# One plan of slots for the attention work between the matmuls of blocks 1 to 6

## The chip, the cores and the metric

The kernel runs on one NeuronCore of one Trainium2 chip. The metric is the device time of one execution in microseconds (us). The core has TensorE (PE, the matmuls; PEld is its weight load), VectorE (DVE), ScalarE (ACT), GpSimd (POOL, which here issues the large loads) and SyncE (SP, which here issues transposing DMAs). PSUM is the memory that matmuls write into; it is handed out in pieces called banks.

## The reference, cut to what matters

Two stages follow each other. Linear attention with a cosine weight (8 batches, 8 heads, 576 tokens, head size 64) makes the 4608 x 512 input `x` of a mixture of 8 expert MLPs, of which every token takes all eight, weighted by a normalised routing matrix.

```python
q_p = phi(q, cos_w, sin_w); k_p = phi(k, cos_w, sin_w)   # relu, times cos and sin: 64 -> 128 features
kv  = einsum('bhsf,bhsd->bhfd', k_p, v)                  # "key sums"
z   = sum(k_p, axis=2)                                   # also from the key sums
num = einsum('bhsf,bhfd->bhsd', q_p, kv)
den = einsum('bhsf,bhf->bhs', q_p, z) + 1e-6
attn_out = num / den
# x = attn_out as 4608 x 512
P = exp(x @ w_gate ...); 8 rounds of row and column normalisation
out = sum over e of P[:, e] * (relu(x @ w1[e]) @ w2[e])
```

## The kernel before

While TensorE computes expert 0 for the tokens that are ready, the attention for the next tokens is woven in between. A block `j` is 512 tokens of expert 0: 16 slots, slots 0 to 7 one part of the first layer (`ffn1`, four matmuls of 128x512, about 0.87 us), slots 8 to 15 half a tile of the second (`ffn2`, the same size). After the matmuls of a slot the pieces of attention listed for it are written. The order in which instructions are written is the order on each engine: TensorE, VectorE and ScalarE each run their list in order, and a piece that has to wait holds up all that stands behind it on its engine (the trace of block 3 below shows it: `zsel` starts only at 123.58 us, behind VectorE's earlier pieces).

```python
for slot in range(NS):                      # NS = 16
    ... ffn1(hT, w0, j, [slot])  or  ffn2(...)
    for fn, args in todo.get((j, slot), []):
        fn(*args)
```

In block `j`, batch `b = j + 1` is finished and batch `b + 1` prepared. The pieces, by head pair `hk` (four of them):

```python
def prep_k(b, hk):  # ScalarE: relu(k) in place
def prep_q(b, hk):  # VectorE: relu(q), q_p = q * (cos, sin); from batch 2 on SyncE transposes it by DMA:
        qTs[b, hk] = q_pTs[(b * HK + hk) % len(q_pTs)]
        nc.sync.dma_start(out=qTs[b, hk], in_=q_p[:]..., transpose=True)
def prep_kv(b, hk): # VectorE: k_p = k * (cos, sin), and a copy of v into v_aug
def sums(b, half):  # TensorE: 36 small matmuls k_p x v_aug for two head pairs, into two banks; then sums_made
def sums_made(b, half, kv_ps):
    for hh in range(2):
        ve.tensor_tensor(out=zsel..., in0=zmask..., in1=kv_v[..., D : D + 1]..., op=ALU.mult)   # VectorE reads the bank
        se.copy(out=kv_sb..., in_=kv_v[:, :, 0:D])                                           # ScalarE reads the bank
def denominators(b):# TensorE: 24 matmuls zsel x qT, then VectorE: add, reciprocal, two splits -> hl
def attend(b, hk):  # TensorE: rb_ps = spread(hl) -> ScalarE copies to rb; num_ps = kv_sb x qT -> VectorE: xT = num_ps * rb
def gates(j):       # TensorE: x @ w_gate, ScalarE: exp
def load(b, half, names, held_back)  # GpSimd issues the loads of q, k, v; held_back: not before VectorE's last piece so far
```

All PSUM tiles of these pieces come from one pool of four banks, `small_ps`, taken in turn: two for `sums`, one for `denominators`, four for an `attend`. The plan before had one scheme for blocks 1 and 2 and another from block 3 on:

```python
elif b < B:
    if j <= 2:
        at(j, 0, prep_q, b, 3); at(j, 1, prep_kv, b, 3)
        at(j, 1, sums, b, 0);   at(j, 3, sums, b, 1)
        ...
    else:
        at(j, 0, sums, b, 1)
    at(j, 5 if j <= 2 else 4, denominators, b)
    for hk in range(HK):
        at(j, 8 + 2 * hk, attend, b, hk)
if j:
    at(j, 6, gates, j)
if j <= 1:
    ... load(b + 1, half) at slots 2 * half; prep of b + 1 from slot 6 on, except the fourth q and the fourth k, v
elif b + 1 < B:
    for slot, fn, hk in ((4, prep_k, 0), (5, prep_q, 0), (6, prep_kv, 0), ... (9, prep_q, 3), ... (12, prep_kv, 3)):
        at(j, slot, fn, b + 1, hk)
    at(j, 10, sums, b + 1, 0)
if 1 <= j and b + 2 < B:
    for half in range(2):
        at(j, 10 + half, load, b + 2, half, "qkv", True)
```

`kv_sb` and `zsel` are the two results of a key sum: `kv`, for the numerators, and `z`, masked by head, for the denominators. `rb` holds one over the denominators, spread out, and `xT` the finished attention.

(The `turn` pieces of the printed kernel do nothing from batch 2 on, which is all that these lines reach.)

The softmax here doesn't subtract the row's maximum and nothing guards it: scores larger than these inputs give would overflow.

## Time and profile before

The median is 1005.67 us (1005.21 to 1006.58); the profiled run has a span of 1005.6 us.

| what | before |
|---|---|
| TensorE busy, share of the span | 97% |
| TensorE's share of the chain of waits | 91% |
| blocks 1, 2, 3, 4, 5, 6 | 21.24, 31.49, 21.33, 21.34, 21.33, 18.76 us |
| mean granted clock in block 1, block 2, blocks 3 to 6 | 0.92, 0.84, 1.00 |

The blocks are cut at the first `ffn1` matmul of each in the timeline; only block 1 is cut at its third, the first one after its wait for `xT` (its first stands at 52.29 us). First, two parts of the page: the busy times, and the granted clock of TensorE in 40 slices of 25 us.

```profile
PE 974.6 (97%) x7846; PEld 681.4 (68%) x7846; DVE 810.0 (81%) x1838; ACT 566.3 (56%) x1260; POOL 60.3 (6%) x82
...
PEclk8997999999999999999999999999999999999999
```

The fourth slice (75 to 100 us) stands at 7. The windows view gives one row for each block: stretch, length, then busy time and instructions of PE, PEld, DVE, ACT, POOL, and last the mean clock, the share of the DMA engines and GB/s. Here are blocks 1 to 4.

```profile
53.77:75.01 21.24, 20.89 (x206) 10.09 (x206) 14.48 (x33) 12.42 (x28) 3.41 (x5) 0.92 0.41 61
75.01:106.50 31.49, 23.77 (x241) 11.38 (x240) 17.42 (x41) 13.04 (x32) 4.38 (x7) 0.84 0.82 121
106.50:127.83 21.33, 19.91 (x209) 10.15 (x208) 14.03 (x33) 12.80 (x29) 4.43 (x8) 1.00 0.84 139
127.83:149.17 21.34, 19.92 (x206) 10.06 (x204) 14.03 (x33) 12.79 (x29) 4.31 (x7) 1.00 0.81 139
```

Block 2 is 10 us longer than its neighbours, and blocks 3 and 4 have 1.4 us each in which TensorE has nothing to do. The waits view (engine, line, what it waited for: total us, times, longest) of TensorE up to 195 us names the two largest. L109 is the line of the helper that records every instruction, so one goes by the tiles; `acc_lo<-q_p` and `acc_hi<-q_p` are transposing DMAs of q into two pieces of borrowed storage.

```profile
PE small_ps L109 <- DMA acc_lo<-q_p: 6.4, 1, 6.4
PE small_ps L109 <- ACT kv_sb L109: 4.2, 4, 1.2
...
PE small_ps L109 <- DMA acc_hi<-q_p: 0.5, 1, 0.5
```

The long one is in block 2. The timeline of TensorE there (start, length, engine, instruction, count; in brackets the idle time before it):

```profile
81.85 0.51 PE L109 MATMUL small_ps<-q_pT,zsel 128*32 128x192 f16 x12
88.73 0.51 PE L109 MATMUL small_ps<-acc_lo,zsel 128*32 128x192 f16 x6 [6.38 <-DMA acc_lo<-q_p]
89.72 0.51 PE L109 MATMUL small_ps<-acc_hi,zsel 128*32 128x192 f16 x6 [0.47 <-DMA acc_hi<-q_p]
90.16 1.89 PE L109 MATMUL h_ps<-xT,w1e 128*128 128x512 f16 x4
```

Half of the denominators is done, the rest waits for the transposes of the third (`acc_lo`) and fourth (`acc_hi`) head pairs. SyncE's timeline shows when these were issued, the third just before block 2 begins and the fourth in it:

```profile
74.86 3.24 SPq L339 DMA_TRANSPOSE acc_lo<-q_p  x1
78.27 6.15 SPq L339 DMA_TRANSPOSE acc_hi<-q_p  x1
```

The last row of TensorE's timeline shows the after-effect: four matmuls of 128x512 take 1.89 us, where the usual four take 1.03 as this view counts. What the transposes met is in the DMA view, for issues between 74 and 76 us (last figure: us from issue to landing):

```profile
q_ld<-in_q_dram POOLq DMA_DIRECT2D x1, 288.0 KB, 10.2
k_ld<-in_k_dram POOLq DMA_DIRECT2D x1, 288.0 KB, 12.5
v_ld<-in_v_dram POOLq DMA_DIRECT2D x1, 288.0 KB, 13.4
acc_lo<-q_p SPq DMA_TRANSPOSE x1, 13.8
```

The fourth pair's transpose takes 11.4 us. In block 3 the same transpose as in the last row lands after 3.3 us. The other wait recurs in every block from 2 to 5. In block 3, VectorE, ScalarE and TensorE around 124 us:

```profile
122.55 0.75 DVE L109 TENSOR_TENSOR k_p<-k_ld,acc_hi 128x1152 f16<-128x1152 f16 x1
123.21 0.45 DVE L109 COPY acc_lo<-v_ld 128x576 f16<-128x576 f16 x1
123.58 0.34 DVE L109 TENSOR_TENSOR zsel<-acc_hi,small_ps 128x64 f16<-128x64 f16 x2
...
123.82 0.43 ACT L109 CAST kv_sb<-small_ps 128x128 f16<-128x128 f32 x2 [3.82 <-DVE zsel L109]
...
124.14 0.44 PE L109 MATMUL small_ps<-q_pT,kv_sb 128*64 128x384 f16 x4 [1.21 <-ACT kv_sb L109]
```

VectorE is late with `zsel`, ScalarE's copy waits for `zsel`, and TensorE's `attend` for that copy. The `kv_sb` that the `attend` reads is the one of the current batch, long there; what it lacks is the PSUM bank, which is that of the next batch's key sums.

### The profile page before, as it was taken

The numbers are of one execution on the slowest core, as the hardware profiler recorded it, in microseconds if no ns is written. First come the engines' busy times: TensorE is split into PE (matmuls) and PEld (weight loads), VectorE is DVE, ScalarE is ACT, GpSimd is POOL, SyncE is SP. The second block draws the span as 40 slices with busy tenths as digits, with TensorE's granted clock in tenths as the row PEclk, the third lists the DMA queues.
The fourth block names the chain that finished last, engine by engine and source line by source line (L and its number), as shares of the span: only waits on it lengthen the run. The fifth ranks groups of instructions, "written<-read, shape, count | busy, mean of one in ns | idle before, by whom it ended". The sixth has DMA issues, their size and how long they took to land.

```text
span 1005.6 us, 20219 instructions
## 1 busy us (share of the span) xinstructions
PE 974.6 (97%) x7846; PEld 681.4 (68%) x7846; DVE 810.0 (81%) x1838; ACT 566.3 (56%) x1260; POOL 60.3 (6%) x82
## 2 busy tenths in 40 slices
PE   7997999999999999999999999999999999999997
PEld 7543444445777777777777777777777777777775
DVE  5875665488989887898889878888889888988886
ACT  5653566547777555555555555555555555555551
POOL 6310220001000000000000000000000000000001
PEclk8997999999999999999999999999999999999999
DMA  9947885353101331034013321043113410104535
GB/s 167 205 76 112 143 143 95 71 103 66 49 24 34 81 66 48 25 66 90 25 33 65 61 65 30 24 91 66 30 43 67 83 32 25 48 24 108 132 87 124
DMA packets 80336, 73.54 MB, mean 73 GB/s; under 512 B 33264, under 2 KB 72176, under 8 KB 80240
## 3 DMA queue, kind: packets, MB, share of 16 engines
q0 software_dynamic: 27232, 30.94, 19.5%
q1 hardware_dynamic: 52768, 41.06, 16.6%
q8 instruction: 61, 1.00, 0.4%
q14 instruction: 35, 0.29, 0.1%
q10 hardware_dynamic: 240, 0.26, 0.1%
HBM read 83.12 MB, written 12.98 MB: 96 GB/s over the span
## 4 chain that ended last, share of the span: by engine, by line
PE 91%; DVE 4%; DMA 2%; ACT 1%; issue 1%; POOL 1%; DVEq 0%; POOLq 0%; ACTq 0%; SPq 0%
PE rows_ps L109 33%; PE h_ps L109 27%; PE copied_ps L109 11%; PE p_ps L109 11%; PE y_ps L109 5%; PE small_ps L109 4%; DMA acc_hi<-q_p 1%; DVE xT L109 1%; DMA k_ld<-in_k_dram 1%; DVE k_p L109 1%; DVE den L109 0%; DVE acc_lo L109 0%; ACT rb L109 0%; DVE acc_hi L819 0%; POOL hs_last L834 0%
## 5 line engine op out<-in xcount | busy, mean ns | idle before, releaser
L819 DVE SCALAR_TENSOR_TENSOR acc_lo<-rows_ps,P_tok,acc_lo 128x512 f32<-128x512 f32 (+1 forms) x322 | 203.3, 640 | 74.6 <-PE rows_ps L109 74.5
L109 PEld LDWEIGHTS <-H 128*128 128x128 f16 x2080 | 203.0, 98 | 83.1 <-issue 1.2
L755 ACT CAST u<-h_ps 128x384 f16<-128x384 f32 x288 | 137.8, 478 | 130.6 <-PE h_ps L109 130.0
L109 PEld LDWEIGHTS <-w1e 128*128 128x128 f16 x1632 | 157.0, 98 | 69.1 <-issue 8.8
L749 DVE CUSTOM_DVE_ANT_0 H<-p_ps,u 128x384 f16<-128x384 f32 x329 | 181.2, 551 | 6.7 <-PE p_ps L109 6.5
L109 PEld LDWEIGHTS <-hs 128*128 128x128 f16 x1500 | 146.6, 98 | 56.2
L109 PE MATMUL h_ps<-S,w1e 128*128 128x384 f16 x672 | 164.1, 326 | 1.1 <-ACT u L109 0.9
L109 PE MATMUL p_ps<-xT,T 128*128 128x384 f16 x672 | 164.1, 326 | 0.1
L109 PE MATMUL h_ps<-xT,w1e 128*128 128x384 f16 (+1 forms) x616 | 152.6, 356 | 1.3 <-DVE xT L109 1.2
L109 PE MATMUL rows_ps<-V,H 128*128 128x256 f16 x1000 | 150.0, 273 | 0.7 <-DVE acc_hi L819 0.7
L109 PE MATMUL rows_ps<-w2e,hs 128*128 128x256 f16 x1000 | 150.0, 273 | 0.0
L787 ACT ACTIVATE H<-h_ps 128x384 f16<-128x384 f32 x144 | 70.7, 491 | 95.1 <-PE h_ps L109 95.1
L109 PEld LDWEIGHTS <-T 128*128 128x128 f16 x1008 | 98.1, 98 | 29.2 <-issue 2.8
L109 PE MATMUL rows_ps<-w2e,H 128*128 128x256 f16 (+1 forms) x568 | 91.2, 285 | 0.0
L768 ACT COPY copied_ps<-h_ps 128x384 f32<-128x384 f32 x144 | 67.4, 468 | 35.6 <-PE h_ps L109 35.4
L778 ACT ACTIVATE H<-copied_ps 128x384 f16<-128x384 f32 x144 | 70.9, 492 | 20.3 <-PE copied_ps L109 20.3
L109 PE MATMUL h_ps<-S,T 128*128 128x384 f16 x336 | 81.8, 325 | 0.3 <-ACT copied_ps L109 0.3
L109 PE MATMUL copied_ps<-xT,w1e 128*128 128x384 f16 x336 | 82.1, 326 | 0.0
L109 PE MATMUL copied_ps<-w2e,H 128*128 128x256 f16 x504 | 75.5, 272 | 0.0
L109 PE MATMUL rows_ps<-V,hs 128*128 128x256 f16 x500 | 74.9, 272 | 0.0
L819 DVE SCALAR_TENSOR_TENSOR acc_lo<-copied_ps,P_tok,acc_lo 128x256 f32<-128x256 f32 x126 | 60.2, 477 | 0.4
L819 DVE SCALAR_TENSOR_TENSOR acc_hi<-rows_ps,P_tok,acc_hi 128x512 f32<-128x512 f32 (+1 forms) x56 | 41.3, 737 | 20.1 <-PE rows_ps L109 19.3
(135 smaller groups left out, 962.9 us busy)
## 6 DMA issues: line engine op xcount, KB each, us to landing
S<-x_saved SPq DMA_DIRECT2D x108, 192.0 KB, 2.4
out_dram<-acc_lo SPq DMA_DIRECT2D x62, 128.0 KB, 2.4
w1e<-in_moe_w_dram POOLq DMA_DIRECT2D x7, 1024.0 KB, 9.0
w2e<-in_moe_w_dram POOLq DMA_DIRECT2D x7, 1024.0 KB, 9.6
k_ld<-in_k_dram POOLq DMA_DIRECT2D x16, 288.0 KB, 8.5
v_ld<-in_v_dram POOLq DMA_DIRECT2D x16, 288.0 KB, 9.4
q_ld<-in_q_dram POOLq DMA_DIRECT2D x16, 288.0 KB, 8.6
x_saved<-S SPq DMA_DIRECT2D x18, 192.0 KB, 1.9
```

The costliest lines, as they stand in the source:

```text
L109: i = getattr(self.engine, name)(*args, **kwargs)
L749: latest = ve._custom_dve(TENSOR_ADD_SAT, out=out, in0=ps[:, 0:TU], in1=t[:], s0=FP32_MAX, s1=0.0)
L755: se.copy(out=t[:], in_=ps[:, 0:TU])
L768: se.copy(out=Y[:, 0:TU], in_=X[:, 0:TU])
L778: se.activation(out=h11, in_=Y[:, 0:TU], func=AF.Relu)
L787: se.activation(out=h12, in_=X[:, 0:TU], func=AF.Relu)
L819: ve.scalar_tensor_tensor(out=a, in0=rows, scalar=P_tok[:, g, self.e : self.e + 1], in1=a, op0=ALU.mult, op1=ALU.add,)
```

## The change

One scheme of slots for blocks 2 to 6, and a variant one slot later for the preparation in block 1. Batch 3 is now wholly prepared in block 1, and its first key sum taken there at slot 15. Key sums of the next batch stand at slot 14, behind all attends (before: 10), and at slot 0; denominators at slot 3 (before: 4, in block 2: 5), attends at 6, 8, 10, 12 (before: 8 to 14), gates at 5, held-back loads at 11 and 12. In `sums_made` ScalarE reads first. One more line, left out below, moves the loads of the second half of batch 3 from slot 2 of block 1 to slot 0. The work is the same.

```diff
@@ sums_made
             for hh in range(2):
+                se.copy(out=kv_sb[:, 2 * half : 2 * half + 2, hh, :], in_=kv_v[:, :, 0:D])
                 ve.tensor_tensor(out=zsel[...], in0=zmask[...], in1=kv_v[...], op=ALU.mult)
-                se.copy(out=kv_sb[:, 2 * half : 2 * half + 2, hh, :], in_=kv_v[:, :, 0:D])
@@ the plan (empty turn lines left out)
-                if j <= 2:
+                if j == 1:
                     at(j, 0, prep_q, b, 3)
                     at(j, 1, prep_kv, b, 3)
                     at(j, 1, sums, b, 0)
                     at(j, 3, sums, b, 1)
                 else:
                     at(j, 0, sums, b, 1)
-                at(j, 5 if j <= 2 else 4, denominators, b)
+                at(j, 5 if j == 1 else 3, denominators, b)
                 for hk in range(HK):
-                    at(j, 8 + 2 * hk, attend, b, hk)
+                    at(j, (8 if j == 1 else 6) + 2 * hk, attend, b, hk)
             if j:
-                at(j, 6, gates, j)
+                at(j, 5, gates, j)
...
             elif b + 1 < B:
                 for slot, fn, hk in (
-                    (4, prep_k, 0), (5, prep_q, 0), (6, prep_kv, 0), (6, prep_k, 1),
-                    (7, prep_q, 1), (8, prep_kv, 1), (8, prep_q, 2), (9, prep_k, 2),
-                    (9, prep_q, 3), (10, prep_kv, 2), (11, prep_k, 3), (12, prep_kv, 3),
+                    (3, prep_k, 0), (4, prep_q, 0), (4, prep_k, 1), (5, prep_q, 1),
+                    (7, prep_kv, 0), (7, prep_k, 2), (7, prep_q, 2), (9, prep_q, 3),
+                    (9, prep_k, 3), (9, prep_kv, 1), (11, prep_kv, 2), (13, prep_kv, 3),
                 ):
-                    at(j, slot, fn, b + 1, hk)
-                at(j, 10, sums, b + 1, 0)
+                    at(j, slot + (j == 1), fn, b + 1, hk)
+                at(j, 15 if j == 1 else 14, sums, b + 1, 0)
...
-                    at(j, 10 + half, load, b + 2, half, "qkv", True)
+                    at(j, 11 + half, load, b + 2, half, "qkv", True)
```

## The prediction

> **What bounds the kernel now.** TensorE: the page gives it 97% busy and 91% of the chain of waits. The change touches only the attention stage (up to about 190 us); from 228 to 994 us the windows view shows TensorE 763.79 of 766.00 us busy, so nothing can be won there. Cut at the first expert-layer matmul of each block, the timeline gives block 1 about 53.9 to 75.0, block 2 75.0 to 106.67, blocks 3, 4, 5 21.33 us each, block 6 18.74 us. A block without waits, summed from the timeline (64 matmuls of 128x512 at 0.216 = 13.8; key sums 2 x 0.68; denominators 0.77; gates 0.5; attends 4 x 0.71), is 19.3 us; block 6, which has one key sum, is already there. So block 2 loses about 12 us and blocks 3 to 5 about 1.9 each: 18 us in all is the most to be had, under 2% of 1005.67.
>
> **Where it is lost.**
> 1. Block 2, 6.4 + 0.5 us (waits view): its denominators wait for the DMA transposes of the fourth head pair, whose inputs are made only in this block's slot 0. They take 13.8 and 11.4 us to land (3.2 to 3.3 in steady blocks) because they share the DMA engines with the loads issued at 71.6 to 75.9 us. After this pause matmuls run at half speed (4 in 1.8 us instead of 0.87) until about 96 us, some 4 us more. The Trainium skill ("TensorE: Matmul & The Clock Gate", Part 1) says idling halves the clock[...]; this trace agrees (mean clock 0.84 in block 2, 1.00 in blocks 3 to 5).
> 2. Each of blocks 2 to 5, 0.6 to 1.2 us: an attend waits for ScalarE's copy of the key sums, which waited 3.2 to 3.9 us for VectorE's zsel (0.34), itself queued behind preparation and xT work. Around it another 0.5 us or so (slot 10 sums waiting for banks).
>
> **What the change does.** No work is added or removed (the removed turns were already empty for these blocks). All preparation for block 3 moves into block 1, and one key sum (0.68) with it. The key sums of the next block move behind the attends, ScalarE reads them first, denominators and attends come one to two slots earlier.
>
> **Walking VectorE through the new steady block** with its durations (denominator chain 2.4 from +5.0; q 1.01, k and v 1.04, xT pair 0.73): xT pairs end near +10.2, 13.0, 15.8, 17.5, the last preparation at +18.6; TensorE asks for those banks at about +10.8, 13.3, 15.7. So almost no stall, and 19.4 to 19.7 us a block. The last q transposes are issued near +14, the loads near +17, so they hardly meet.
>
> **Sum.** Block 2: -12.0; blocks 3 to 5: 3 x -1.8; block 1: +0.8 (key sum, small waits); prologue and block 0: +0.5, as VectorE's zsel now waits for a busier ScalarE there (up to 1.3 us later, mostly hidden); residual waits +0.5. Total about -15.6: **990 us**, 8 in 10 between 986.8 and 996. Chances: faster by over 2% 0.04, within 2% 0.94, slower 0.02.
>
> **Right or wrong will show as:** no wait of small_ps on q_p transposes at block 2; no half-speed matmuls there; blocks 2 to 5 each below 19.8 us; kv_sb no longer waiting on zsel; 228 us onward the same length.
>
> **What would break it:** the loads, issued about as late as before while the first k relu moves one slot earlier, may land after ScalarE needs them (k lands near +3.7 of the next block, needed at +4.6); ScalarE would hold back the FFN's relu and TensorE. Transposes of block 1 could still meet the loads. VectorE may run later than I reckon and starve the banks of the attends.

## The result, and the profile after

The median is 989.58 us (989.15 to 991.7, four runs) against 1005.66 in the same rounds; the ratio is 0.9843, 95% interval 0.9826 to 0.986. Ratios here are the mean time of one kernel's runs over that of the other's of the same rounds, so not quite the ratio of the quoted medians. That is 1.6% faster, and 0.4 us from the forecast.

The page's clock row has lost its dip in the fourth slice:

```profile
PE 968.0 (98%) x7846; PEld 677.9 (69%) x7846; DVE 810.4 (82%) x1838; ACT 566.4 (57%) x1260; POOL 60.4 (6%) x82
...
PEclk8999999999999999999999999999999999999999
```

The windows view, blocks 1 to 4 again:

```profile
53.57:74.52 20.95, 20.30 (x242) 10.22 (x242) 16.79 (x39) 13.17 (x29) 2.33 (x4) 1.00 0.63 86
74.52:94.16 19.64, 19.64 (x210) 9.74 (x205) 15.23 (x36) 12.61 (x31) 4.29 (x7) 1.00 0.96 154
94.16:113.81 19.65, 19.65 (x210) 9.84 (x209) 14.10 (x32) 12.74 (x29) 4.32 (x7) 1.00 0.91 151
113.81:133.44 19.63, 19.63 (x205) 9.71 (x204) 14.10 (x32) 12.74 (x29) 4.29 (x7) 1.00 0.91 154
```

TensorE's busy time in blocks 2 to 4 is now the length of the block. (The counts differ between rows because some matmul records are missing from a trace.) Block by block:

| | before | after | difference |
|---|---|---|---|
| start to block 1 | 53.77 | 53.57 | -0.20 |
| block 1 | 21.24 | 20.95 | -0.29 |
| block 2 | 31.49 | 19.64 | -11.85 |
| blocks 3, 4, 5 | 64.00 | 58.93 | -5.07 |
| block 6 | 18.76 | 18.75 | -0.01 |
| the rest | 816.34 | 815.56 | -0.78 |
| span | 1005.6 | 987.4 | -18.2 |

The two profiled spans differ by more than the medians (16.1 us): the execution profiled before took 1007.32 us, 1.7 above its median, and the one after 989.15, 0.4 below. Block 1 accounts for some 1 us of this (see "The changed kernel again"). The last row but one is no work of TensorE's: from the end of block 6 to VectorE's last instruction it is 811.62 us before and 811.66 after, and the 0.8 us lie behind that. They do not look like chance: the other five kernels below that keep the old read order and the old slots from block 3 on (`sums14` but for its key sums) have 816.3 to 816.4 us there; `swap_only` and `steady_only` have 815.6, as have all three profiles of the changed kernel. What shortens the end of the program was not tried. The waits for `q_p` transposes and for `kv_sb` are gone from TensorE's list up to 195 us; its two largest entries now are of the start-up:

```profile
PE small_ps L109 <- DVE k_p L109: 2.9, 1, 2.9
PE small_ps L109 <- ACT acc_lo L109: 1.5, 1, 1.5
```

The denominators of block 2, without a gap, and the matmuls behind them at full speed (eight in 1.90 us):

```profile
78.86 0.51 PE L109 MATMUL small_ps<-q_pT,zsel 128*32 128x192 f16 x12
79.20 0.34 PE L109 MATMUL small_ps<-acc_lo,zsel 128*32 128x192 f16 x6
79.37 0.34 PE L109 MATMUL small_ps<-acc_hi,zsel 128*32 128x192 f16 x6
79.63 1.90 PE L109 MATMUL h_ps<-xT,w1e 128*128 128x512 f16 x8
```

And the two readers of the key sums, at the end of block 4, in the new order; VectorE now waits for ScalarE, and nobody for either:

```profile
132.67 0.43 ACT L109 CAST kv_sb<-small_ps 128x128 f16<-128x128 f32 x2 [0.95 <-PE small_ps L109]
...
132.97 0.39 DVE L109 TENSOR_TENSOR zsel<-acc_hi,small_ps 128x64 f16<-128x64 f16 x2 [0.38 <-ACT kv_sb L109]
```

### The profile page after: what moved, and what is told of

It is laid out like the page before. It is cut to its first block, busy times and chain, and to the rows that moved or that the text cites. A ratio compares the mean times of both kernels' runs of the same rounds, so it can differ in the third digit from the quotient of the medians. Undisturbed runs are those within 1.5% of the kernel's fastest.

```text
span 987.4 us, 20228 instructions
## 1 busy us (share of the span) xinstructions
PE 968.0 (98%) x7846; PEld 677.9 (69%) x7846; DVE 810.4 (82%) x1838; ACT 566.4 (57%) x1260; POOL 60.4 (6%) x82
## 4 chain that ended last, share of the span: by engine, by line
PE 93%; DMA 2%; DVE 2%; ACT 1%; POOL 1%; issue 0%; DVEq 0%; POOLq 0%; ACTq 0%; SPq 0%
PE rows_ps L109 34%; PE h_ps L109 28%; PE copied_ps L109 11%; PE p_ps L109 11%; PE y_ps L109 5%; PE small_ps L109 4%; DMA v_ld<-in_v_dram 2%; DMA q_pT<-q_p 1%; DVE xT L109 0%; DVE acc_hi L814 0%; POOL hs_last L829 0%; DVE P_tok L109 0%; DMA out_dram<-acc_lo 0%; DVE colp L109 0%; ACT u L109 0%
## 5 line engine op out<-in xcount | busy, mean ns | idle before, releaser
L109 PE MATMUL h_ps<-xT,w1e 128*128 128x384 f16 (+1 forms) x616 | 150.3, 351 | 1.4 <-DVE xT L109 1.3
```

The costliest lines, as they stand in the source:

```text
L109: i = getattr(self.engine, name)(*args, **kwargs)
```

## The experiments

Twelve experiments ran, in three groups of four: ten edited kernels, and the changed kernel twice more. The ratio of each is to the kernel before in the same group. The theory: (1) block 2's 12 us come from transposes that share the DMA engines with the loads of batch 4, and from the half-speed clock after that pause; (2) the 1.7 us a block in blocks 3 to 5 come from where the key sums stand between the attends. Rivals: the transposes are simply issued too late; the read order does it.

### The changed kernel again

No edit, twice more.

> The changed kernel once more, beside the others of this group. Expected ratio to the kernel before 0.984 (989 to 992 us); a second profile shows how much of the first one's 18.2 us of span is luck of the clock in block 1 (mean clock 0.92 before, 1.00 after in the first profiles): if it is luck, block 1 can show a clock below 1.00 here.

> The changed kernel again, as the other side of the comparison with the second try at block 0. Expected ratio 0.9835 to 0.9845. A third profile for the luck of the clock at the start of block 1: the first five matmuls after the waits there took 1.24 us or 2.29 us in the profiles so far, in both kernels.

Measured: 989.88 us (989.51 to 990.58, ratio 0.9837) and 989.39 us (989.29 to 990.43, ratio 0.9836). The result stands in each of the three groups in which the changed kernel ran. The second profile does show the slow start of block 1: there the changed kernel has its first five matmuls in 2.29 us, in the first profile in 1.24, and the kernel before in 1.94.

```profile
54.50 1.94 PE L109 MATMUL h_ps<-xT,w1e 128*128 128x512 f16 x5 [0.35 <-DVE xT L109]
```

```profile
54.29 1.24 PE L109 MATMUL h_ps<-xT,w1e 128*128 128x512 f16 x5 [0.35 <-DVE xT L109]
```

```profile
54.88 2.29 PE L109 MATMUL h_ps<-xT,w1e 128*128 128x512 f16 x5 [0.31 <-DVE xT L109]
```

The third profile has 1.24 us again. So part of one profile is chance: block 1 took 21.80 us in the second profile of the changed kernel against 20.95 in the first and 20.49 in the third. Its cost is best read where the clock stayed at 1.00. With the old plan of block 1 it took 19.72 us in five experiments (`early_loads`, `sums14`, `steady_only`, `no_loads4`, `loads_mid`), and with the new one 20.49 or 20.50 in three (`plan_no_swap`, `block1_only`, the third profile): 0.77 us more, as it should be with a key sum of 0.68 more. The slow clock adds 1.5 us to the old block 1 (21.24) and 1.3 to the new (21.80).

### The slots without the read order, and the read order without the slots

```diff
 # plan_no_swap: the changed kernel, sums_made as before
-                se.copy(out=kv_sb[...], in_=kv_v[:, :, 0:D])
                 ve.tensor_tensor(out=zsel[...], ...)
+                se.copy(out=kv_sb[...], in_=kv_v[:, :, 0:D])
 # swap_only: the kernel before, sums_made as after
+                se.copy(out=kv_sb[...], in_=kv_v[:, :, 0:D])
                 ve.tensor_tensor(out=zsel[...], ...)
-                se.copy(out=kv_sb[...], in_=kv_v[:, :, 0:D])
```

> The new slots, but VectorE reads the key sums first as before. Theory (the slots carry the gain, the read order is worth almost nothing once the key sums stand behind the attends): within 1 us of the changed kernel, blocks 3 to 5 at 19.6 to 19.8 us each. Rival (the read order frees ScalarE's copy and with it the attends): the kernel loses at least 1 us in each of blocks 2 to 5, so 993.5 us or more.

> The kernel before with only the read order turned round. Theory: the wait in blocks 2 to 5 is for a bank of the key sums, which now VectorE's zsel frees last, still queued behind preparation; so only the 0.3 us that the ScalarE copy took after zsel is won, blocks 3 to 5 near 21.0 us, 1003.5 to 1005.5 us in all, block 2 unchanged. Rival (read order decisive): blocks 3 to 5 near 20.0 us, 1000 to 1002 us in all.

Measured: without the read order 989.08 us (987.25 to 990.93), ratio 0.9829 (0.9811 to 0.9847), beside 0.9837 (0.9823 to 0.985) for the whole change in the same group; blocks 3 and 4 take 19.64 and 19.63 us. The read order is worth nothing that these times can show once the slots are changed (in the profile block 2 takes 19.81 us without it and 19.64 with it). Alone it gives 1003.7 us, ratio 0.9979 (0.9965 to 0.9992), and blocks 3 to 5 of 21.03 us instead of 21.33. Of its 2.1 us that is 0.9; some 0.75 is the shorter end of the program told of above, and block 2 gives 0.4. The waits view of the swapped kernel says why so little: the same bank is now released by the other late reader.

```profile
PE small_ps L109 <- DMA acc_lo<-q_p: 6.3, 1, 6.3
PE small_ps L109 <- DVE zsel L109: 2.7, 3, 0.9
```

Both readers must have finished before TensorE gets the bank. Whichever of the two goes first, the slower queue (here VectorE's) decides.

### The two parts apart

`block1_only` is the kernel before with batch 3 prepared in block 1; `steady_only` has the new slots from block 3 on and the new read order.

```diff
 # block1_only (empty turn lines left out)
-                if j <= 2:
+                if j == 1:
-                at(j, 5 if j <= 2 else 4, denominators, b)
+                at(j, 5 if j == 1 else 4, denominators, b)
 # preparation in block 1 at the change's slots, from block 2 on at the old ones
-                at(j, 10, sums, b + 1, 0)
+                at(j, 15 if j == 1 else 10, sums, b + 1, 0)
-                    at(j, 10 + half, load, b + 2, half, "qkv", True)
+                    at(j, (11 if j == 1 else 10) + half, load, b + 2, half, "qkv", True)
 # steady_only
-                at(j, 5 if j <= 2 else 4, denominators, b)
+                at(j, 5 if j <= 2 else 3, denominators, b)
-                    at(j, 8 + 2 * hk, attend, b, hk)
+                    at(j, (8 if j <= 2 else 6) + 2 * hk, attend, b, hk)
 # gates, preparation, key sums and loads likewise: the new slots for j > 2
```

> The kernel before, with only this of the change: batch 3 is prepared wholly in block 1 and its first key sum taken there, loads for batch 4 one slot later in block 1. From block 2 on the old slots and the old read order. Theory (the change has two separate parts, and this one is the transposes of block 2): no wait for transposes in block 2, full clock there, block 2 like the old blocks 3 to 5 (21.3 us instead of 31.5), block 1 0.7 us longer: 995 to 998 us. Rival (the old slots of block 2 still make their own long wait): block 2 stays above 24 us.

> The kernel before, with only the other part: from block 3 on the new slots, and the new read order everywhere; blocks 1 and 2 at the old slots. Theory: blocks 3 to 5 fall from 21.33 to about 19.7 us each, block 2 keeps its 6 us wait for transposes: 1000 to 1002 us. With the other part (and about 1.7 us more that block 2 itself gets from the new slots) the two add up to the whole change. Rival (the parts need each other): under 2 us gained.

Measured: `block1_only` 997.69 us, ratio 0.9909 (0.9895 to 0.9922); `steady_only` 1001.09 us, ratio 0.9943 (0.9929 to 0.9956). Block 2 of the first and block 3 of the second, from the windows view:

```profile
74.88:96.22 21.34, 19.92 (x209) 10.05 (x205) 14.69 (x35) 12.56 (x31) 5.58 (x9) 1.00 0.91 153
```

```profile
105.99:125.63 19.64, 19.64 (x209) 9.84 (x208) 14.22 (x33) 12.74 (x29) 3.15 (x6) 1.00 0.85 137
```

Both are what the theory named, 21.3 and 19.7. The gains add: 0.91% and 0.57% are 1.48% of the whole change's 1.57 to 1.64%. The rest, 0.9 to 1.6 us, is no larger than what these intervals leave open (over 1 us each); the profiles show better where it lies: block 2 itself gets 1.70 us from the new slots (21.34 against 19.64), which neither part has.

### Key sums at slot 14 alone

```diff
-                at(j, 10, sums, b + 1, 0)
+                at(j, 14, sums, b + 1, 0)
```

> The kernel before with one number changed: the first key sums of the next batch at slot 14, not 10 (blocks 2 to 6); denominators, attends, preparation and read order as before. Theory (the key sums between the attends take their banks and put zsel in VectorE's queue between the xT products): the waits for kv_sb go, a wait of about 0.5 us a block for xT at the third attend stays, blocks 3 to 5 at 20.0 to 20.5 us, 1001 to 1003 us. Rival (it is the earlier denominators and attends that win the steady blocks): blocks 3 to 5 stay above 21 us.

Measured: 1004.36 us, ratio 0.9972 (0.9956 to 0.9987). The time is 1.4 us above the expected range (the kernel before had a median of 1006.78 in this group, 1.1 above its first one), but the blocks are near where they were put: 20.60 and 20.57 us for blocks 3 and 4, 0.1 above the range. Moving the key sums is worth 0.75 of the 1.7 us a block; so the second half of the theory, that the place of the key sums makes the 1.7 us, holds for less than half of it. The rest comes with the other slots that moved (denominators, attends, preparation). The waits for `kv_sb` did go. The wait that was expected to stay is there, at the third attend:

```profile
118.94 0.44 PE L109 MATMUL small_ps<-q_pT,kv_sb 128*64 128x384 f16 x4 [0.54 <-ACT rb L109]
```

The view puts it down to ScalarE's `rb`, but VectorE's pair of `xT` products started at 118.48 and took 0.82 us for two, so the first of them released its bank just before 118.94; it is the likelier releaser. The attend needs both.

### Are the transposes late, or slowed?

Three tries, all on the kernel before, with the transposes of the third and fourth head pairs of batch 3 left at the end of block 1 and in block 2.

```diff
 # early_loads: the loads of batch 4 at slots 5 and 6 of block 1
-                    at(j, 10 + half, load, b + 2, half, "qkv", True)
+                    at(j, (5 if j == 1 else 10) + half, load, b + 2, half, "qkv", True)
 # loads_mid: at slot 3 of block 1
+                    at(j, 3 if j == 1 else 10 + half, load, b + 2, half, "qkv", True)
 # no_loads4: none (wrong results on purpose, for batch 4)
+                if b == 4:
+                    i = nc.gpsimd.memset(x[:]..., 0.1)
+                else:
                     i = nc.gpsimd.dma_start(...)
```

> The kernel before with one edit: in block 1 the loads for batch 4 start at slots 5 and 6, not 10 and 11, so they are nearly done when the last transposes of batch 3 are issued in block 2, which stay where they were. Theory (contention with those loads makes the transposes late): they land in 3 to 5 us, the wait for them in block 2 falls from 6.9 us to under 1 us, TensorE keeps its full clock, 994 to 997 us. Rival (they are simply issued too late, or slow in that place): wait of 5 us or more stays, 1003 to 1006 us.

> The kernel before with the six loads of batch 4 replaced by fills of the same tiles with 0.1 (wrong results for that batch, on purpose): the traffic is gone, every other instruction stands where it stood, and the last transposes of batch 3 are still issued in block 2. The first try at this (loads at slots 5 and 6) only moved the collision onto earlier transposes, which then held their buffers. Theory (contention): both transposes land in 3 to 4 us, no wait for them in block 2 over 1 us, full clock, block 2 at 21 to 22 us, 994.5 to 998 us. Rival (too late in the program whatever else runs): the wait stays at 5 us or more, above 1002 us.

> The kernel before with the loads of batch 4 at slot 3 of block 1 (start near 60.5 us), correct results: the loads then run from about 60.5 to 72 us, and meet only the first two transposes of batch 3, not the last two. Theory (contention): the last two land in 3 to 5 us and the wait in block 2 falls to at most 1 us, unless the first two are so late that they hold the buffers of the fourth as in the earlier try; 995 to 999 us if they are not. Rival: wait of 5 us or more, above 1002 us.

The first was a miss: 1004.14 us, ratio 0.9983 (0.9966 to 1.0). The loads then started at 65.02 us, just before the transpose of the first head pair at 65.82, and this one took as long as the last ones had:

```profile
65.82 12.73 DMA q_pT<-q_p
78.55 0.03 issue
...
78.64 0.76 DVE q_p L109
```

These are lines of the chain of waits: VectorE could not write the fourth `q_p` until 78.64, because `q_p` has three buffers and the transpose that was reading one landed only at 78.55. The delay had moved, not gone; the last two transposes still took 8.6 and 5.8 us, TensorE waited 0.35 and 2.18 us for them, and block 2 took 28.42 us.

The other two kept the loads away altogether. With fills in their place the two transposes land in 3.2 us each, there is no wait for them, the clock in block 2 is 1.00, and the time is 998.71 us, ratio 0.9924 (0.9907 to 0.994), 0.7 us above the expected range; block 2 takes 23.62 us, where 21 to 22 was expected. It keeps both of its key sums and its old slots. With the loads at slot 3 (59.65 to 63.96 us, as issued) the results are right and the time is 997.77 us, ratio 0.9916 (0.9901 to 0.9931). Its DMA view, for issues from 73 to 76 us and from 76 to 79 us, and its block 2:

```profile
acc_lo<-q_p SPq DMA_TRANSPOSE x1, 3.2
...
acc_hi<-q_p SPq DMA_TRANSPOSE x1, 3.2
```

```profile
73.53:96.51 22.98, 20.87 (x242) 10.75 (x241) 17.34 (x41) 13.03 (x32) 3.49 (x5) 1.00 0.55 102
```

The transposes are issued where they were, so they were not too late; it is the loads that slow them, and one number in the old plan (3 for 10) takes away 8.5 us of block 2. The Trainium skill ("Trainium Kernel Development and Optimization", Key Constraints) says that DMAs from the SP, ACT and POOL queues run on the same 16 DMA engines and interleave. This agrees, and gives the price: 3.2 us alone, 11.4 to 13.8 us beside the six loads of a batch. That the shared engines are the reason, and not something else that loads and transposes share, is the page's account; the runs show only that the loads do it.

### Two tries to do better

The changed kernel still waits about 2.5 us between the last attends of block 0 and the start of block 1. Both edits are on the changed kernel.

```diff
 # tuned
-            if g % 2 == 0 or TCH // P <= g < (B - 1) * TCH // P:
+            if g % 2 == 0 or g < (B - 1) * TCH // P:
-                    at(j, 11 + i // 2, fn, b + 1, hk)
+                    at(j, 15 if i > 5 else 11 + i // 2, fn, b + 1, hk)
 # tuned2: the second edit, and
+            if g % 2 == 0 or 3 <= g < (B - 1) * TCH // P:
-                    at(j, 0, prep_q, b, 3)
-                    at(j, 1, prep_kv, b, 3)
+                    at(j, 0, prep_kv, b, 3)
                     at(j, 1, sums, b, 0)
+                    at(j, 1, prep_q, b, 3)
```

> The changed kernel with two edits in block 0, where TensorE still waits about 2.5 us for VectorE's xT at the end of the block: the two result copies that VectorE made there go to ScalarE, and the preparation of slot 14 moves behind the last attends of slot 15. If those waits are VectorE's queue alone, they fall under 1 us and the kernel is 1 to 2.5 us faster than the changed one (987.5 to 989 us). If ScalarE or the loads then bind, it stays within 0.5 us of it or gets slower.

> The changed kernel with block 0 mended better than in the first try: only the last result copy goes to ScalarE, two preparations move behind the last attends, and the fourth k and v preparation of batch 2 goes before the fourth q (the first try had left a new wait of 1 us for it). Expected: waits of TensorE between the last attends of block 0 and slot 3 of block 1 under 0.8 us in all (2.5 in the changed kernel), 1 to 2 us faster than the changed kernel in the same group.

Measured: `tuned` 989.18 us, ratio 0.9826 (0.9812 to 0.9839); it ran in another group than the changed kernel, whose ratios are 0.9843, 0.9837 and 0.9836, two inside that interval and one 0.0004 above it: not distinguishable. Its waits for `xT` at the start of block 1 are gone, but there is a new one of 0.97 us for the copy of v (`acc_lo`) in block 1. `tuned2` 990.6 us, ratio 0.9845 (0.983 to 0.986), beside 0.9836 in the same group: no better. It removes the two waits at the start of block 1 (0.99 and 0.35 us), but 0.74 and 0.28 us remain at the last attends of block 0, and it gets to the denominators of block 1 before the transpose that it had put later. The forecast of under 0.8 us in all was a miss:

```profile
61.01 0.35 PE L109 MATMUL small_ps<-q_pT,zsel 128*32 128x192 f16 x6 [1.65 <-DMA q_pT<-q_p]
...
61.80 2.77 PE L109 MATMUL h_ps<-xT,w1e 128*128 128x512 f16 x8
```

A 1.65 us wait, and the next eight matmuls at a falling clock (2.77 instead of 1.90 us). Neither version beats the changed kernel.

## Why the prediction was right, point by point

- *Size.* Forecast 990 us, measured 989.58. That it lies well inside the range is due to block 6, whose 18.76 us had no idle time and showed what a block without waits costs; this put a ceiling of 18 us on the gain, under 2% of the whole. That it agrees to 0.4 us is partly luck: blocks 2 to 5 gave 16.92 us of the 17.4 forecast, and of the 1.8 us of costs forecast only the 0.77 of block 1 were found.
- *Block 2, forecast -12.0.* Measured -11.85. The cause, loads in the way of transposes, is shown by the kernels with the loads moved or left out. One detail was wrong: the prediction speaks of the fourth head pair alone, made in slot 0 of block 2. The transpose of 13.8 us, for which TensorE waited 6.4 of the 6.9 us, is the third pair's, issued at 74.86 us before block 2 began; the fourth's landed about 1 us later (78.27 and 11.4), so it would have held TensorE alone as well. The change brings both forward (68.73 and 71.02 us in the profile after, landing in 3.5 and 3.2 us), so the forecast did not suffer. The half-speed clock is in the trace: TensorE's busy time in block 2 falls from 23.77 to 19.64 us for a work that is one key sum smaller.
- *Blocks 3 to 5, forecast -1.8 each at 19.4 to 19.7 us.* Measured -1.69 each, at 19.64. The walk through VectorE's queue held: it put the ends of the `xT` pairs at 10.2, 13.0, 15.8, 17.5 us after the block's start, and block 4 of the profile after has them at 10.5, 13.2, 16.0 and 17.7 (last product's end less 113.81).
- *Block 1, forecast +0.8.* +0.77 between the profiles in which the clock stayed at 1.00 (20.49 against 19.72). The first pair of profiles shows -0.29, because the one before had the slow clock there (1.5 us) and the one after took 0.46 us longer than the other full-clock profiles of this plan, 0.29 of it a wait for `xT` at the last attend.
- *Start-up and block 0, forecast +0.5.* Not seen. VectorE's `zsel` did wait for ScalarE there (2.29 and 1.18 us in the timeline after), but from block 0's first `h_ps` matmul to block 1's five-matmul group after the waits it is 28.83 us in both kernels. This term was mis-sized: in block 0 its cost on TensorE is 0.0. For the start-up that stays open, because block 0's first `h_ps` matmul stands anywhere from 23.75 to 27.29 us in the 14 profiles.
- *The loads.* The risk named did not come: in block 4 the k load issued at 112.20 us landed 5.0 us later, at 117.2, and ScalarE took it up at 118.73 without waiting.
- *The read order.* The prediction listed it beside the slots without a size. By the runs it is worth about 0.3 us a block in the old plan and nothing that the times show in the new.
- *228 us onward, forecast the same length.* It is for TensorE and VectorE; the 0.8 us by which the program ends sooner were not foreseen and are not explained.
- *Left open.* What divides the remaining 0.95 us a block between earlier denominators, earlier attends and the new order of preparation was not tried apart.

## What to carry to other kernels

Where many small pieces are woven into a stream of matmuls, put a piece whose PSUM banks will be released late behind the pieces that would otherwise wait for those banks, and look at which in-order queue releases a bank last, not at who reads it first. A DMA that must land in time should not be issued next to bulk loads: ask what else is in flight before calling it late. And cost a block without waits from its own matmuls first: it says how much a better plan can win at most.

## What the Trainium skill lacked or had wrong

- "Trainium Kernel Development and Optimization", Key Constraints, says that the queues' DMAs interleave; it has no size for what that does to a transpose. Here: 3.2 us alone, 11.4 to 13.8 us beside six loads of a batch, with the same transpose in the same place back at 3.2 us when the loads were moved.
- "TensorE: Matmul & The Clock Gate", Part 1, has the half-speed clock come after an idle window of about 3.4 us. The pause in block 2 agrees (idle from about 82.3 us, clock at 0.90 in the stretch 84 to 86 us and at 0.50 from 86). But at the start of block 1 the clock fell to half in three of the twelve profiles in which block 0 is not edited (the kernel before, the second of the changed kernel, the swapped one) with no single wait above 1 us: in the kernel before TensorE was busy 1.60, 1.26 and 1.12 us of each 2 us from 48 to 54. The same page names short idle times as a second way to the same end, without a figure for how much idling it takes.
- The same part has the full clock back after about 3.4 us of work. Here in block 2 work began again at 88.73 us and ran on without a gap from 89.72; the clock was at 0.54 in the stretch from 94 to 96 us and at 1.00 from 96, over 6 us later. This need not contradict the page: it also says that the window runs freely, so that up to two windows, 6.8 us (an estimate from its figure), can pass before one is full. The trace does not show the windows.
- "PSUM — Partial Sum Buffer", Terms, has two engines that read one bank at once as an error, and says the compiler keeps them apart. In the traces shown here one reader waits for the other, in the written order (ScalarE for VectorE 3.82 us before, VectorE for ScalarE 0.38 us after). The page does not say what follows for a plan: the order of the two readers matters little (0.3 us a block in the old plan), and what counts is when the later one is done.
